# Adding up a guard's counts on VectorE after a small DMA, in place of an FP32 matmul on TensorE

## The chip, the cores and the metric

The kernel runs on one core of one Trainium2 chip. The metric is device time in microseconds (us) of one execution, and the figure given is the median over several runs. A profile of one execution stands beside it; its times count from the first to the last recorded instruction of the core (the span).

## What is computed

For 4 batches, 8 heads, 768 positions and a head width of 64 the reference does windowed attention with four sink positions and passes the result, with the heads side by side (512 columns), through a normalised two-layer block:

```python
scores = scale * np.matmul(q, k.transpose(0, 1, 3, 2))
keep = is_sink | in_window          # 4 sinks, a window of 128
a = np.exp(scores - max); a = a / (sum(a) + 1e-09)
x = np.matmul(a, v)                 # to [4, 768, 512]
xn = (x - mu) / np.sqrt(var + 1e-06) * g_ln
out = x + np.maximum(xn @ w_ch1, 0.0) @ w_ch2   # 512 -> 2048 -> 512
```

## The kernel before

**Tiles and stages.** The 3072 rows of the output are 24 tiles of 128 rows (`NT`), two of which make a chunk (`NC` = 12 chunks). Each tile is attended (scores L980, exponentials L998, values L953 to L969, reciprocals of the row sums L1021), normalised (L881 to L891) and transposed by a DMA (L577). Each chunk then goes through the two layers in `mlp(c)`: eight groups of first-layer matmuls `ph` (L1046), each followed by a ReLU on ScalarE (L1056), then for each tile i of the chunk sixteen second-layer matmuls `pc` in four groups `pc{t}{f}_{s}` (L1074), a VectorE instruction `o{t}{f}` that scales the sum and adds x (L1083), and a store of the tile to HBM, `st{t}{f}` (L1087). The last tile, 23, is cut into two halves of 256 columns: the first half's store is issued by ScalarE, the second half's by SyncE, and that one is the last store of the program (`order_last`, L1132).

**The guard.** The exponentials are taken without subtracting the row maximum, so a check runs at the end: `guard` (L1114 to L1116, VectorE) looks at all 24 x 8 reciprocals of each of the 128 partitions and leaves one count per partition in `n_bad`, 128 x 1. `gsum` (L1119) adds the 128 counts with an FP32 matmul against a column of ones, on TensorE, into one element of PSUM; `gflag` (L1121, VectorE) turns that element into the integer `flag`. At the end every engine reads `flag` into a register (`values_load`, L1159) and branches (L1161): over zero, the whole computation is done again by a slow general path; at zero, which is what happens here, the program ends. The last store on SyncE is put behind SyncE's read of the flag (L1160). `hold` (L1125) is a small FP32 matmul behind the last `o`.

**What sets the order.** Every step is an operation of `Plan` with a cost on each engine that may do it, a priority, and the buffers that it reads and writes. `Plan.run` plays the operations through with these costs and writes down the order of each engine; the instructions are then emitted in that order (L1152 to L1160), and each engine runs its own list in order. `gsum` has the priority `16.0 * NC + 0.7`, which puts it into the second-layer matmuls of tile 22, between the first and the second group of four (`pc220_0` and `pc220_1`). The four PSUM buffers `one` are shared by `ph`, `pc`, `gsum` and `hold` as they come free.

**Completion counters of DMAs.** Each DMA that SyncE or ScalarE issues takes the next of eight completion counters in turn, 0 to 7 and then 0 again; a consumer waits on the counter of its DMA. In the kernel before, the last few are: transpose of tile 23 counter 2, store of tile 20 counter 3, of tile 21 counter 4, of tile 22 counter 5, first half of tile 23 counter 6, second half 7.

**The end of the program.** After its branch SyncE goes through twelve waits, one instruction each, before it reports to the barrier that closes the program; in the profile they are the EVENT_SEMAPHORE rows of SyncE at L1196. Waits 1 to 4 name the counters of the GpSimd DMAs, two at a time. Waits 5 to 12 name the hardware DMA counters 0, 1, 2, ... 7 in this order, each beside a counter of an engine.

Of the kernel before, what the change touches and what calls it, by code (L numbers as in the profile page):

```python
# [7 lines left out]
FP32 = mybir.dt.float32  # L8
BF16 = mybir.dt.bfloat16
AF = mybir.ActivationFunctionType  # L10
ALU = mybir.AluOpType
# [185 lines left out]
def pe(us):  # L197
    return {"PE": (us, us + Plan.PE_DRAIN)}


def act(n):
    t = 0.065 + 0.000833 * n
    return (t, t + 0.105)


def dve(n, per=1.04):
    t = 0.067 + 0.001 * per * n
    return (t, t + 0.09)


def fix(occ, extra=0.09):
    return (occ, occ + extra)
# [10 lines left out]
HW_T = (0.10, 0.8, 0.8)  # L223
# [146 lines left out]
def kernel(  # L370
# [12 lines left out]
    nc = tc.nc  # L383
# [10 lines left out]
    NT = B * RB  # L394
    NC = B * RC
# [7 lines left out]
    P = Plan()  # L403
# [26 lines left out]
    def const(name, shape, dtype):  # L430
        return consts.tile(shape, dtype, name=name)
# [14 lines left out]
    w2 = [const(f"w2_{c}", [128, 4, DM], BF16) for c in range(4)]  # L446
    junk = nc.const_aps.tensor(1.0, [128, 512], BF16)
    rec, low = const("rec", [128, NT, H], FP32), const("low", [128, NT, H], FP32)
    n_bad, flag = const("n_bad", [128, 1], FP32), const("flag", [1, 1], mybir.dt.int32)
    g_s, g_r = const("g_s", [128, H, NS], FP32), const("g_r", [128, 3, H], FP32)  # L450
    ones_f = const("ones_f", [128, 1], FP32)
# [3 lines left out]
    Bc = {n: Buf(n) for n in names}  # L455
# [4 lines left out]
    def constant(name, eng, us, prio, emit, reads=(), **kw):  # L460
        return P.op(name, {eng: fix(us)}, prio, emit, reads=[Bc[r] for r in reads], **kw)

    V, G = nc.vector, nc.gpsimd
# [4 lines left out]
        out=ident_f, in_=ident_f, compare_op=ALU.not_equal, fill=1.0, base=0,  # L468
        pattern=[[-1, 128]], channel_multiplier=1), rw=[Bc["ident_f"]])
    constant("up1", "POOL", 0.3, -98, lambda e: G.affine_select(  # L470
        out=upper, in_=upper, compare_op=ALU.is_ge, fill=0.0, base=0,
# [36 lines left out]
    def negs(e):  # L508
# [7 lines left out]
        out=sel.rearrange("p (a b h) -> p a b h", a=2, b=2),  # L516
        in_=ident.rearrange("p (a b t h s) -> p t a b h s", a=2, b=2, h=2, s=NS)[:, 0],
        op=ALU.add, axis=mybir.AxisListType.X), ["ident"], writes=[Bc["sel"]])
# [8 lines left out]
         writes=[gr_b], dma=HW_T)  # L527
    P.op("gtt", pe(0.1), PAR["gtt"], lambda e: nc.tensor.transpose(gt_p.t[:, 0:NDM], g_rows, ident_f[0:NDM, 0:NDM]),
         reads=[gr_b, Bc["ident_f"]], writes=[gt_p])
    P.op("gtc", {"DVE": fix(0.07)}, PAR["gtt"] + 0.1, lambda e: V.tensor_copy(gt, gt_p.t[:, 0:NDM]), reads=[gt_p], writes=[Bc["gt"]])  # L530
    for h in range(H):
# [3 lines left out]
            reads=[Bc["vc"]], writes=[Bc["vcd"]], nb=3.5 + 0.55 * h)  # L535
    for b in range(B):
# [4 lines left out]
            reads=[Bc["vcd"], Bc["vc"], Bc["sel4" if b else "sel"]], writes=[Bvs[b]], nb=PAR["vs0"][1] if b == 0 else 40.0 * b)  # L541
# [7 lines left out]
    for c in range(4):  # L549
        sl = slice(512 * c, 512 * (c + 1))  # L550
        P.op(f"w1ld{c}", {"POOL": (0.75, 0.8)}, w1prio[c], lambda e, c=c, sl=sl: G.dma_start(
            w1[c], moe_w_ch1[:, sl].rearrange("(j p) n -> p j n", p=128)), writes=[Bw1[c]], dma=SW_W)
    for c in range(4):
        P.op(f"w2ld{c}", {"POOL": (0.75, 0.8)}, PAR["w2p"][c], lambda e, c=c: G.dma_start(
            w2[c], moe_w_ch2[512 * c:512 * (c + 1), :].rearrange("(t p) n -> p t n", p=128)),
            writes=[Bw2[c]], dma=SW_W)
# [471 lines left out]
    def mlp(c):  # L1028
        T = 16.0 * c + 8.0
        xnt = xnt_b[c]  # L1030
        h1 = []
        by_tile = c < PAR["by_tile"]
        for u in range(NH1 // 2):
            ph, hb = Buf(f"ph{c}_{u}", "one"), Buf(f"h{c}_{u}", "h1")

            def mm_t(e, u=u, ph=ph):
                for s in range(4):
                    for j in range(NDM):
                        nc.tensor.matmul(ph.t[:, 128 * s:128 * s + 128], lhsT=w1[u // 2][:, j, 128 * s:128 * s + 128],  # L1039
                                         rhs=xnt.t[:, j, 128 * (u % 2):128 * (u % 2) + 128], start=j == 0, stop=j == NDM - 1)  # L1040

            def mm(e, u=u, ph=ph):
                for s in range(2):
                    ht = 2 * u + s
                    for j in range(NDM):
                        nc.tensor.matmul(ph.t[:, 256 * s:256 * s + 256],  # L1046
                                         lhsT=w1[ht // 4][:, j, 128 * (ht % 4):128 * (ht % 4 + 1)],
                                         rhs=xnt.t[:, j, :], start=j == 0, stop=j == NDM - 1)
            pr = T + u + 0.5
            o = P.op(f"ph{c}_{u}", pe(0.944 if by_tile else 0.872), pr, mm_t if by_tile else mm, reads=[xnt_t[2 * c + u % 2] if by_tile else xnt, (Bw1 if c < PAR["x_by_dma"] else Bw1g)[u // 2]],  # L1050
                     writes=[ph], hold=[hb, xnt])
            last_use[u // 2] = [o]

            def rl(e, ph=ph, hb=hb):
                if e == "ACT":
                    nc.scalar.activation(hb.t, ph.t, AF.Relu)  # L1056
                else:
                    V.tensor_scalar_max(hb.t, ph.t, 0.0)
            P.op(f"rl{c}_{u}", {"ACT": act(512), "DVE": dve(512)}, pr - 3, rl, reads=[ph], writes=[hb])
            h1.append(hb)  # L1060
        T += 8
        for i in range(2):
            t = 2 * c + i
            b, r = t // RB, t % RB
            ot, st, rs, x = Buf(f"ot{t}", "ot"), xst_b[t], xst_b[t, "rs"], x_b[t]
            cuts = LAST_CUTS if t == NT - 1 else (0, DM)
            for f in range(len(cuts) - 1):
                pc, wd = Buf(f"pc{t}{f}", "one"), cuts[f + 1] - cuts[f]
                sl = slice(cuts[f], cuts[f + 1])
                for s in range(4):  # L1070
                    def mm(e, s=s, i=i, pc=pc, sl=sl, wd=wd):
                        for ii in range(4):
                            ht = 4 * s + ii
                            nc.tensor.matmul(pc.t[:, 0:wd],  # L1074
                                             lhsT=(h1[2 * s + i].t[:, 128 * ii:128 * ii + 128] if by_tile else
                                                   h1[ht // 2].t[:, 256 * (ht % 2) + 128 * i:256 * (ht % 2) + 128 * i + 128]),
                                             rhs=w2[s][:, ii, sl], start=ht == 0, stop=ht == NH1 - 1)
                    P.op(f"pc{t}{f}_{s}", pe(0.865 * wd / DM), T + 4 * i + s + 4 * f + 0.5, mm,
                         reads=[*([h1[2 * s + i]] if by_tile else h1[2 * s:2 * s + 2]), Bw2[s]], **({"writes": [pc]} if s == 0 else {"rw": [pc]}))
                oo = Buf(f"oo{t}{f}")  # L1080
                tail["ot"], tail["oo"] = ot, oo
                P.op(f"o{t}{f}", {"DVE": dve(wd, 1.14)}, T + 4 * i + 3.5, lambda e, sl=sl, pc=pc, wd=wd, ot=ot, st=st, x=x:
                     V.scalar_tensor_tensor(ot.t[:, sl], in0=pc.t[:, 0:wd], scalar=st.t[:, 16:17],  # L1083
                                            in1=x.t[:, sl], op0=ALU.mult, op1=ALU.add),
                     reads=[pc, st, rs, x], writes=[ot, oo])
                P.op(f"st{t}{f}", {"ACT" if len(cuts) - f in LAST_ACT else "SP": (0.54, 0.59)}, T + 4 * i + 3.6,
                     lambda e, sl=sl, ot=ot, b=b, r=r: (nc.sync if e == "SP" else nc.scalar).dma_start(  # L1087
                         out[b, 128 * r:128 * (r + 1), sl], ot.t[:, sl]),
                     reads=[ot, oo], dma=HW_S)

    last_use, tail = {}, {}
# [11 lines left out]
    for c in range(NC):  # L1103
        mlp(c)
        if c == PAR["x_by_dma"] - 1:
            for s in range(4):
                for j in range(NDM):
                    P.op(f"w1g{s}{j}", {"DVE": fix(0.26), "ACT": act(512)}, 16.0 * c + PAR["w1g"] + 2 * s + 0.1 * j,
                         lambda e, s=s, j=j: V.tensor_scalar_mul(w1[s][:, j, :], w1[s][:, j, :], gt[:, j:j + 1]) if e == "DVE" else
                         nc.scalar.mul(w1[s][:, j, :], w1[s][:, j, :], gt[:, j:j + 1]),  # L1110
                         reads=[Bw1[s], Bc["gt"]], writes=[Bw1g[s]], after=last_use[s])

    def guard(e):
        V.tensor_scalar(low, rec, LOW, HIGH, op0=ALU.max, op1=ALU.min)  # L1114
        V.tensor_tensor(low, low, rec, op=ALU.not_equal)
        V.tensor_reduce(out=n_bad, in_=low, op=ALU.add, axis=mybir.AxisListType.XY)  # L1116
    nb_b, pt_f, fl_b = Buf("n_bad"), Buf("ptf", "one"), Buf("flag")
    P.op("guard", {"DVE": fix(0.9)}, 1000.0, guard, reads=recs, writes=[nb_b])
    P.op("gsum", pe(0.06), 16.0 * NC + 0.7, lambda e: nc.tensor.matmul(  # L1119
        pt_f.t[0:1, 0:1], lhsT=n_bad, rhs=ones_f, start=True, stop=True), reads=[nb_b, Bc["ones_f"]], writes=[pt_f])  # L1120
    P.op("gflag", {"DVE": fix(0.1)}, 1000.0, lambda e: V.tensor_copy(flag, pt_f.t[0:1, 0:1]),  # L1121
         reads=[pt_f], writes=[fl_b])

    hl = Buf("hold", "one")
    P.op("hold", pe(0.06), 1000.0, lambda e: nc.tensor.matmul(  # L1125
        hl.t[0:1, 0:1], lhsT=tail["ot"].t[:, DM - 1:DM], rhs=ones_f, start=True, stop=True),
        reads=[tail["ot"], tail["oo"], Bc["ones_f"]], writes=[hl])
# [5 lines left out]
    t = PAR["t0"]  # L1133
    for o in order:
# [6 lines left out]
        if n > 0:  # L1141
            free = [(max([e_ for b_, e_ in banks[i].lives if b_ < t], default=0.0), i) for i in range(8)
                    if all(e_ < t or b_ > o.start + 0.3 for b_, e_ in banks[i].lives)]
            if free:
                i = min(free)[1]
                sizes = [512] * (n // 2) + [256] * (n % 2) if cold else [256] * n
                items.append((t + 0.001, -1, (sizes, pairs[i // 2][:, i % 2, :] if i < 4 else ones[i - 4])))
        t = o.start + occ * (2 if cold and not o.name.startswith("pm") else 1)
# [52 lines left out]
```

## Time and profile before

| what | value |
|---|---|
| median of 3 runs | 216.78 us (216.47 to 216.9) |
| the profiled execution's own time | 217.02 us |
| its span, first to last instruction | 215.5 us |
| TensorE busy / VectorE busy | 205.9 us / 115.3 us |
| granted TensorE clock | 1.000 |

Views of the profile used below: the page (busy times, the chain of work that ended last), the chain in order of time, the timeline (start, duration, engine, line, operation, with neighbouring instructions of a kind merged; a narrow stretch of time shows them nearly one by one), one line's instructions with their durations (min/median/max in ns) and their first and last start, and the DMA view. PE is TensorE's matmuls, PEld its weight loads, DVE VectorE, ACT ScalarE, POOL GpSimd, SP SyncE; a q behind a name is that engine's sequencer, where DMA issues, waits, register loads and branches are found. A matmul's duration includes its way through the array, so matmuls overlap in the records and their rate is read from their starts.

### The profile page before, as it was taken

The numbers are of one execution on the slowest core, as the hardware profiler recorded it, in microseconds if no ns is written. First come the engines' busy times: TensorE is split into PE (matmuls) and PEld (weight loads), VectorE is DVE, ScalarE is ACT, GpSimd is POOL, SyncE is SP. The second block draws the span as 40 slices with busy tenths as digits, with TensorE's granted clock in tenths as the row PEclk, the third lists the DMA queues.
The fourth block names the chain that finished last, engine by engine and source line by source line (L and its number), as shares of the span: only waits on it lengthen the run. The fifth ranks groups of instructions, "written<-read, shape, count | busy, mean of one in ns | idle before, by whom it ended". The sixth has DMA issues, their size and how long they took to land.

```text
span 215.5 us, 6660 instructions
## 1 busy us (share of the span) xinstructions
PE 205.9 (96%) x2743; PEld 144.1 (67%) x2765; DVE 115.3 (53%) x315; ACT 110.0 (51%) x178; POOL 111.8 (52%) x166
## 2 busy tenths in 40 slices
PE   7798899999999999999999999999999999999994
PEld 2467875765865875864865865864865865865853
DVE  5589875698445446446345446446355345444011
ACT  3796387496562562562562562562562562530610
POOL 7978632499972881871971981871971211201000
PEclk9999999999999999999999999999999999999999
DMA  5999999999999999799799899899799302202103
GB/s 156 187 190 205 193 206 192 167 180 132 154 187 169 123 125 145 87 175 151 123 115 170 112 147 145 111 122 168 111 141 149 80 3 76 73 0 76 49 2 105
DMA packets 104554, 28.04 MB, mean 130 GB/s; under 512 B 94788, under 2 KB 101576, under 8 KB 104520
## 3 DMA queue, kind: packets, MB, share of 16 engines
q0 software_dynamic: 69872, 13.18, 90.2%
q1 hardware_dynamic: 33448, 13.74, 35.7%
q10 hardware_dynamic: 1200, 0.66, 1.1%
q8 instruction: 22, 0.36, 0.7%
q14 instruction: 12, 0.10, 0.2%
HBM read 27.43 MB, written 6.29 MB: 156 GB/s over the span
## 4 chain that ended last, share of the span: by engine, by line
PE 88%; DVE 5%; DMA 3%; issue 2%; ACT 1%; ACTq 0%; DVEq 0%
PE one L1074 39%; PE one L1046 36%; PE pair L980 3%; DMA natf<-in_q_dram 3%; PE one L953 2%; PE one L960 2%; PE one L969 1%; DVE st L881 1%; DVE xnt L909 1%; PE one L988 1%; PE one L1039 1%; DVE x L873 1%; DVE xc L885 1%; PE pair L605 1%; PE pair L730 1%
## 5 line engine op out<-in xcount | busy, mean ns | idle before, releaser
L1074 PE MATMUL one<-w,h 128*128 128x512 bf16 (+1 forms) x378 | 84.5, 371 | 2.2 <-issue 1.6
L1056 ACT ACTIVATE h<-one 128x512 bf16<-128x512 f32 x93 | 55.6, 598 | 47.3 <-PE one L1046 42.6
L1046 PE MATMUL one<-xnt,w 128*128 128x256 bf16 x704 | 79.3, 273 | 0.0
L1046 PEld LDWEIGHTS <-w 128*128 128x128 bf16 x704 | 68.6, 98 | 10.4
L1074 PEld LDWEIGHTS <-h 128*128 128x128 bf16 x400 | 37.3, 98 | 39.6
L998 ACT ACTIVATE pe<-pair 128x768 bf16<-128x768 f32 x36 | 27.2, 809 | 41.0 <-PE pair L980 41.0
L645 POOL DMA_DIRECT2D vn<-in_v_dram x59 | 38.7, 695 | 10.9 <-DMA w<-in_moe_w_ch_dram 6.8
L890 POOL TENSOR_SCALAR st<-st 128x1 f32<-128x1 f32 x24 | 8.9, 369 | 62.4 <-DVE st L883 61.9
L1021 DVE RECIPROCAL rec<-one 128x4 f32<-128x4 f32 x36 | 6.4, 178 | 62.5 <-PE one L969 51.1
L1083 DVE SCALAR_TENSOR_TENSOR ot<-one,st,x 128x512 f32<-128x512 f32 (+1 forms) x25 | 18.2, 727 | 13.9 <-PE one L1074 9.0
L891 POOL TENSOR_TENSOR st<-st,mhalf 128x1 f32<-128x1 f32 x24 | 17.0, 707 | 2.0
L881 DVE BATCH_NORM_STATS2 st<-x 128x6 f32<-128x512 bf16 x24 | 16.7, 695 | 0.8
L1023 DVE TENSOR_TENSOR x<-one,rec 128x256 bf16<-128x256 f32 x36 | 15.3, 425 | 1.2
L703 POOL DMA_DIRECT2D nat<-in_k_dram x16 | 14.9, 932 | 1.9 <-DMA natp<-in_q_dram 1.6
L703 POOL DMA_DIRECT2D nat<-in_q_dram x16 | 14.3, 905 | 0.0
L1003 DVE TENSOR_TENSOR pe<-pe,band 128x768 bf16<-128x768 bf16 x24 | 12.2, 552 | 0.0
L885 DVE TENSOR_SCALAR xc<-x,st 128x512 bf16<-128x512 bf16 x24 | 9.3, 387 | 0.9
L980 PE MATMUL pair<-qT,kT 64*64 64x128 bf16 (+1 forms) x528 | 9.2, 204 | 0.0
L953 PEld LDWEIGHTS <-pe 128*128 128x128 bf16 (+1 forms) x144 | 6.2, 97 | 2.9 <-issue 0.8
L778 ACT ACTIVATE pe<-pair 128x1024 bf16<-128x1024 f32 (+1 forms) x8 | 7.1, 916 | 1.8 <-PE pair L730 1.4
L1039 PE MATMUL one<-xnt,w 128*128 128x128 bf16 x128 | 8.0, 220 | 0.0
L980 PEld LDWEIGHTS <-kT 64*64 64x64 bf16 x528 | 7.2, 108 | 0.4 <-ACT w L1110 0.4
(112 smaller groups left out, 165.7 us busy)
## 6 DMA issues: line engine op xcount, KB each, us to landing
out_dram<-ot SPq DMA_DIRECT2D x23, 256.0 KB
w<-in_moe_w_ch_dram POOLq DMA_DIRECT2D x8, 512.0 KB, 14.5
nat<-in_k_dram POOLq DMA_DIRECT2D x16, 128.0 KB, 5.1
nat<-in_q_dram POOLq DMA_DIRECT2D x16, 128.0 KB, 5.6
vn<-in_v_dram POOLq DMA_DIRECT2D x44, 32.0 KB, 6.0
vn<-in_v_dram POOLq DMA_DIRECT2D x15, 64.0 KB, 6.3
natp<-in_k_dram POOLq DMA_DIRECT2D x3, 256.0 KB, 14.3
vn<-in_v_dram POOLq DMA_DIRECT2D x6, 128.0 KB, 9.2
```

Of the source, the lines that this page charges most:

```text
L645: P.op(f"vld{t}_{i}", {"POOL": (0.8, 0.85)}, prio + 0.001 * i, lambda e, p0=p0, n=n, hs=hs, src=src: G.dma_start(m.t[p0:p0 + n, hs, 0:64], ...
L703: lambda e, nat=nat, ap=ap: G.dma_start(nat.t, ap), writes=[nat], dma=SW, after=gate(c))
L881: P.op(f"bn{t}", {"DVE": fix(0.60)}, d + 0.12, lambda e: V.bn_stats(st.t[:, 8:14], x.t), reads=[x], writes=[st, mv])
L891: G.tensor_tensor(st.t[:, 16:17], st.t[:, 17:18], mhalf, op=ALU.pow)),
L980: nc.tensor.matmul(pps[u].t[64 * g:64 * g + 64, h2, col + c0:col + c0 + n], lhsT=kt.t[rs, hp, k0:k0 + 64], rhs=qT.t[rs, hp, q0:q0 + n], st ...
L998: nc.scalar.activation(pes[j].t.rearrange("p a b -> p (a b)")[:, 0:768].rearrange("p (a b) -> p a b", a=2), pps[j].t[:, :, 0:384], AF.Exp, ...
L1003: V.tensor_mul(at_s, at_s, band[j] if r > 1 else edge[r][j].unsqueeze(1).to_broadcast([128, 4, 192]))
L1023: P.op(f"x{t - 1}{u}", {"DVE": dve(256)}, d + 0.051 + 0.002 * u, lambda e, u=u, rc=rc, pv=pv: V.tensor_tensor(x.t[:, 256 * u:256 * u + 256 ...
L1046: nc.tensor.matmul(ph.t[:, 256 * s:256 * s + 256], lhsT=w1[ht // 4][:, j, 128 * (ht % 4):128 * (ht % 4 + 1)], rhs=xnt.t[:, j, :], start=j ...
L1056: nc.scalar.activation(hb.t, ph.t, AF.Relu)
L1074: nc.tensor.matmul(pc.t[:, 0:wd], lhsT=(h1[2 * s + i].t[:, 128 * ii:128 * ii + 128] if by_tile else h1[ht // 2].t[:, 256 * (ht % 2) + 128 ...
L1083: V.scalar_tensor_tensor(ot.t[:, sl], in0=pc.t[:, 0:wd], scalar=st.t[:, 16:17], in1=x.t[:, sl], op0=ALU.mult, op1=ALU.add),
```

## The change

The matmul `gsum` goes. A DMA `gmove`, issued by SyncE, carries the 128 counts from 128 partitions into 128 neighbouring elements of one partition, and `gflag` becomes two VectorE instructions: a reduction of these 128 elements and the conversion to an integer. The new `gflag` is ordered behind `o220`, the VectorE step of tile 22 (`tail["sum", NT - 2]`).

```diff
+    n_bad_t, n_sum = const("n_bad_t", [1, 128], FP32), const("n_sum", [1, 1], FP32)
...
-                P.op(f"o{t}{f}", {"DVE": dve(wd, 1.14)}, T + 4 * i + 3.5, lambda e, sl=sl, pc=pc, wd=wd, ot=ot, st=st, x=x:
+                tail["sum", t] = P.op(f"o{t}{f}", {"DVE": dve(wd, 1.14)}, T + 4 * i + 3.5, lambda e, sl=sl, pc=pc, wd=wd, ot=ot, st=st, x=x:
...
-    P.op("gsum", pe(0.06), 16.0 * NC + 0.7, lambda e: nc.tensor.matmul(
-        pt_f.t[0:1, 0:1], lhsT=n_bad, rhs=ones_f, start=True, stop=True), reads=[nb_b, Bc["ones_f"]], writes=[pt_f])
-    P.op("gflag", {"DVE": fix(0.1)}, 1000.0, lambda e: V.tensor_copy(flag, pt_f.t[0:1, 0:1]),
-         reads=[pt_f], writes=[fl_b])
+    nt_b = Buf("n_bad_t")
+    P.op("gmove", {"SP": (0.54, 0.59)}, 1000.0, lambda e: nc.sync.dma_start(n_bad_t[0:1, :], n_bad[:, 0:1]),
+         reads=[nb_b], writes=[nt_b], dma=HW_T)
+
+    def total(e):
+        V.tensor_reduce(out=n_sum, in_=n_bad_t, op=ALU.add, axis=mybir.AxisListType.X)
+        V.tensor_copy(flag, n_sum)
+    P.op("gflag", {"DVE": fix(0.2)}, 1000.0, total, reads=[nt_b], writes=[fl_b], after=[tail["sum", NT - 2]])
```

In the built program the rest of every engine's list keeps its order. TensorE loses the one instruction at L1119, and the two halves of tile 23 move to another PSUM buffer each. On SyncE `gmove` stands between the transpose of tile 23 and the store of tile 20; on VectorE the two new instructions stand between `o220` and `o230`, where one stood before between `o210` and `o220`. As `gmove` takes counter 3, each later store takes the next counter: tile 20 counter 4, 21 counter 5, 22 counter 6, the first half of tile 23 counter 7, the second half counter 0.

More of the change, by code (lines that the diff above doesn't have):

```diff
@@ L1116, in guard @@
         V.tensor_reduce(out=n_bad, in_=low, op=ALU.add, axis=mybir.AxisListType.XY)
-    nb_b, pt_f, fl_b = Buf("n_bad"), Buf("ptf", "one"), Buf("flag")
+    nb_b, fl_b = Buf("n_bad"), Buf("flag")
     P.op("guard", {"DVE": fix(0.9)}, 1000.0, guard, reads=recs, writes=[nb_b])
-    P.op("gsum", pe(0.06), 16.0 * NC + 0.7, lambda e: nc.tensor.matmul(
-        pt_f.t[0:1, 0:1], lhsT=n_bad, rhs=ones_f, start=True, stop=True), reads=[nb_b, Bc["ones_f"]], writes=[pt_f])
-    P.op("gflag", {"DVE": fix(0.1)}, 1000.0, lambda e: V.tensor_copy(flag, pt_f.t[0:1, 0:1]),
-         reads=[pt_f], writes=[fl_b])
+    nt_b = Buf("n_bad_t")
[5 more added lines that the diff above has]
+    P.op("gflag", {"DVE": fix(0.2)}, 1000.0, total, reads=[nt_b], writes=[fl_b], after=[tail["sum", NT - 2]])
     hl = Buf("hold", "one")
```

## The prediction

> **What bounds the kernel now.** I read the page first, its busy times and its chain of work that ended last:
>
> ```profile
> span 215.5 us, 6660 instructions
> PE 205.9 (96%) x2743; PEld 144.1 (67%) x2765; DVE 115.3 (53%) x315; ACT 110.0 (51%) x178; POOL 111.8 (52%) x166
> ...
> PE 88%; DVE 5%; DMA 3%; issue 2%; ACT 1%; ACTq 0%; DVEq 0%
> ```
>
> TensorE is busy for 96% of the span and carries 88% of the chain. Whatever is taken out of TensorE's list moves all that follows it, so the next view is the chain in order of time, its last pieces (start, us, what):
>
> ```profile
> 205.09 0.22 PE one L1074
> 205.31 0.05 issue
> 205.36 0.60 PE one L1074 x2
> 205.96 0.12 PE one L1119 x2
> 206.07 6.20 PE one L1074 x44
> ...
> 212.37 0.50 DVE ot L1083
> ```
>
> The removed matmul, L1119, lies on the chain. Behind it come 6.20 us of matmuls without a gap, then VectorE's last instruction, then the last store. The end after that store does not appear in the chain as pieces of its own, so I looked up what SyncE does there, at L1196 (count, durations in ns, first and last start). The rows are those of four stretches of time: all until 214.5, until 214.06, from 214.06 to 214.5, and behind 214.5.
>
> ```profile
> L1196 SPq EVENT_SEMAPHORE  x11: 28/28/28, 213.8 to 214.4; - x11
> ...
> L1196 SPq EVENT_SEMAPHORE  x4: 28/28/28, 213.8 to 214.0; - x4
> ...
> L1196 SPq EVENT_SEMAPHORE  x7: 28/28/28, 214.1 to 214.4; - x7
> ...
> L1196 SPq EVENT_SEMAPHORE  x1: 28/28/28, 214.6 to 214.6; - x1
> L1196 SPq DRAIN  x1: 13/13/13, 214.7 to 214.7; - x1
> ```
>
> These are the twelve closing waits. Eleven start between 213.8 and 214.4, ten steps in 0.6 us: 0.06 us for one, although there is nothing left to wait for in them. The twelfth comes at 214.6, some 0.1 us later than this rhythm would bring it. By the program it names counter 7, that of the last store, so it is the one that really waits. The drain follows a step later and the barrier closes the program at 215.5. So the end is: last matmul, VectorE, last store, its landing, and then **no** further wait, because the store's counter stands last in the row.
>
> **What the removed matmul costs.** The chain puts down 0.12 us for it. The starts of its neighbours tell more. The timeline in narrow stretches:
>
> ```profile
> 205.36 0.60 PE L1074 MATMUL one<-w,h 128*128 128x512 bf16 x2
> ...
> 205.57 0.38 PE L1074 MATMUL one<-w,h 128*128 128x512 bf16 x1
> 205.88 0.09 PEld L1119 LDWEIGHTS one<-ones_f,n_bad 128*1 128x1 f32 x2 [0.42 <-ACT h L1056]
> 205.88 0.19 PE L1119 MATMUL one<-ones_f,n_bad 128*1 128x1 f32 x2
> ...
> 206.01 0.60 PE L1074 MATMUL one<-w,h 128*128 128x512 bf16 x2
> ...
> 206.01 0.82 PE L1074 MATMUL one<-w,h 128*128 128x512 bf16 x3
> ```
>
> Two merged matmuls last 0.60 and three 0.82, so one more costs 0.22; the starts 205.36 and 205.57 say 0.21. The matmul behind 205.57 was therefore due at 205.79 and starts at 206.01: **0.22 us lost**, nearly twice the 0.12 of the chain. The row puts the idle time ahead of L1119 down to a ReLU of L1056; I take that label for a coincidence, since by the program L1119 needs a PSUM buffer that an older ReLU, two before the last, has read.
>
> What is late next once it goes? The last ReLU and VectorE's steps:
>
> ```profile
> 205.19 0.60 ACT L1056 ACTIVATE h<-one 128x512 bf16<-128x512 f32 x1 [0.28 <-PE one L1046]
> ...
> 206.11 0.15 DVE L1121 CAST flag<-one 1x1 int32<-1x1 f32 x1 [7.16 <-PE one L1119]
> 208.86 0.75 DVE L1083 SCALAR_TENSOR_TENSOR ot<-one,st,x 128x512 f32<-128x512 f32 x1 [2.61 <-PE one L1074]
> 210.72 0.48 DVE L1083 SCALAR_TENSOR_TENSOR ot<-one,st,x 128x256 f32<-128x256 f32 x1 [1.11 <-PE one L1074]
> 212.37 0.48 DVE L1083 SCALAR_TENSOR_TENSOR ot<-one,st,x 128x256 f32<-128x256 f32 x1 [1.16 <-PE one L1074]
> ```
>
> The last ReLU ends at 205.79. Its first reader is the fifteenth of tile 22's sixteen matmuls; at 0.215 each from 204.93 on it is due at 207.9, two microseconds later. So nothing takes the place of the gap, and I take the whole 0.22 us, with 0.12 as the lower bound. The three VectorE steps each wait for PE and come 0.22 earlier: 208.64, 210.50, 212.15.
>
> **What is added, and what hides it.** First the DMA. On SyncE it stands behind the transpose of tile 23 and ahead of the store of tile 20; it needs the counts of L1116:
>
> ```profile
> 193.75 1.20 SPq L577 DMA_TRANSPOSE xnt<-xc  x1
> ...
> 194.32 0.35 DVE L1116 TENSOR_REDUCE n_bad<-low 128x1 f32<-128x192 f32 x1
> 194.74 0.75 DVE L1083 SCALAR_TENSOR_TENSOR ot<-one,st,x 128x512 f32<-128x512 f32 x1
> ...
> 195.52 0.34 SPq L1087 DMA_DIRECT2D out_dram<-ot  x1
> ```
>
> The counts are there at 194.67, the transpose has been issued at 194.95, and the store waits for VectorE until 195.49. Issuing a store of 128 rows takes 0.34 us and fits into that hole of 0.54. The longest issue among the stores bounds it from above; then the store of tile 20 would start 1.0 us late, with nobody waiting for it before the end. The transpose is ahead of the new DMA and keeps its place.
>
> ```profile
> L1087 SPq DMA_DIRECT2D out_dram<-ot x24: 332/337/1519, 41.1 to 212.9; - x24
> ...
> w<-in_moe_w_ch_dram POOLq DMA_DIRECT2D x8, 512.0 KB, 14.5
> ...
> vn<-in_v_dram POOLq DMA_DIRECT2D x44, 32.0 KB, 6.0
> ```
>
> When does it land? No such DMA, 128 runs of four bytes between partitions, is in this trace. The nearest by size is the 32 KB load, 6.0 us from issue to landing in a busy stretch; the slowest of all is a weight load, 14.5 us. VectorE reaches the reduction at 209.39 (208.64 + 0.75), so from 195.0 there are 14.4 us of cover. Even the slowest would be a bare 0.1 us late, inside the next gap. I cost it at nothing.
>
> The rule in the Trainium skill that speaks against this change is in "DMA: Bandwidth & Descriptors", section "Anatomy of one DMA — SWDGE (gpsimd) path": any DMA, however small, pays some 2 us, most of it for completion. By it the sum, if the DMA stood on the chain, would be 1.8 us worse; behind 14 us of cover it changes nothing, and no row of this trace times so small a transfer.
>
> Then VectorE's two instructions. The reduction lies between the conversion's 0.15 us and the 0.35 us of L1116, which reads 192 elements per partition where this one reads 128; I take 0.3. With the conversion and two steps to start them it makes about 0.5 us, from 209.4 to 209.9, and `o230` is not due before 210.50. Should it run over, `o230` may be late by 1.1 us more before it touches `o231` at 212.15. Nothing again.
>
> The flag is thereby late, at 209.9 and no longer at 206.3. Its readers:
>
> ```profile
> L1159 POOLq TENSOR_LOAD <-flag x1: 498/498/498, 206.3 to 206.3; - x1
> L1159 SPq TENSOR_LOAD <-flag x1: 516/516/516, 210.0 to 210.0; - x1
> ...
> L1159 ACTq TENSOR_LOAD <-flag x1: 473/473/473, 211.7 to 211.7; - x1
> L1159 DVEq TENSOR_LOAD <-flag x1: 546/546/546, 212.4 to 212.4; - x1
> L1159 PEldq TENSOR_LOAD <-flag x1: 490/490/490, 212.9 to 212.9; - x1
> ```
>
> SyncE read it at 210.0, behind the store of tile 22, and has some 2 us before its last store, started at 212.9 in the row of the stores and due at 212.7 now. It does not feel the difference. ScalarE, VectorE and TensorE read later still. Only GpSimd moves, by 3.6 us; that is a rival below.
>
> **What is moved: the counter of the last store.** The added DMA takes a counter, so the last store's is no longer 7 but 0, and 0 is named in the fifth closing wait, not the twelfth. SyncE now comes to the fifth wait at 213.86 (the first of the seven in the row from 214.1, less 0.22), stands there until the store has landed, and only then walks through the seven waits that are left, at 0.06 each, satisfied or not. The store itself lands 0.22 us earlier. The sum from the landing on:
>
> - landing earlier: -0.22
> - seven waits behind it, 7 x 0.06: +0.42 (by rounding of the rows between 0.35 and 0.49)
> - together **+0.20 us**: the drain at 214.9 where it was 214.7, the end at 215.7.
>
> Between ends this is +0.13 to +0.37. On the profiled execution's own 217.02 us it gives 217.22; this execution is 0.24 over the median of the runs shown, 216.78, and the difference carried over makes 216.98. I forecast **217.0 us**: the gain on TensorE is real and is handed back in the closing waits.
>
> **The rivals.** *The full gain arrives.* If waits that are already satisfied cost nothing behind one that has blocked, or the counter order does not hold the end, the time is 216.78 - 0.22 = 216.56. For it: the chain shows the 0.22 plainly. Against it: eleven waits with nothing to wait for took 0.06 each in the rows above.
>
> *The gap on TensorE stays.* If the 0.22 us were a wait for something that the next matmul meets as well, only the closing waits would be left: 216.78 + 0.42 = 217.20. For it is the label of the row, which names a ReLU; against it, that the matmuls behind ran on at once while the last ReLU had ended at 205.79, before L1119.
>
> *GpSimd closes the program late.* This is the one that ends slower:
>
> ```profile
> L1196 POOLq EVENT_SEMAPHORE  x4: 17/17/17, 214.8 to 215.4; - x4
> L1196 POOLq DRAIN  x3: 44/103/1380, 208.3 to 215.3; - x3
> ...
> L1161 POOLq INC_SWDGE_SEM  x1: 512/512/512, 207.8 to 207.8; - x1
> ```
>
> From its read of the flag at 206.3 GpSimd needs until 208.3 + 1.38 = 209.7, which is 3.4 us, then it waits for the others until 214.8. Started at 209.9 it is done at 213.3, with 1.7 us to spare before the 215.0 that my sum needs. It decides once the stretch grows by more than 1.7 us, and from there on each microsecond is one on the end: with the drain and the semaphore step (1.38 and 0.51) twice as long beside the stores it would be 217.2, with the whole stretch twice as long 218.7. Against it: the same steps run on the same idle engine, and nothing else was behind them before.
>
> **How the numbers follow.** 0.2% is 0.43 us, about what a measurement of this kernel can tell from no change (three runs spread from 216.47 to 216.9). Forecast, +0.20: 0.68. Full gain, -0.22: 0.14. Gap stays, +0.42: 0.08. GpSimd late, mostly by over half a microsecond: 0.10. The first two lie within the bound but for the spread of a measurement; the third lies on its edge, the fourth beyond. Slower by over 0.2%: 0.10, half of 0.08, and 0.06 out of the forecast's tail, 0.20. Faster: 0.05, out of the full gain's tail. Within: 0.75. The range takes in the full gain at its lower end and the nearer part of the late GpSimd at its upper: 216.45 to 217.45.
>
> **What would show it.** In the profile after: L1074 without a gap between its fourth and fifth matmul of tile 22, and VectorE's last three steps 0.2 us earlier; the last store issued at 212.7; on SyncE five closing waits up to about 214.4, with a gap before the fifth, and seven behind it at 0.06; GpSimd's read of the flag at 209.9 and its drain done by 213.5. The forecast is wrong if the twelfth wait follows the landing at once, or if `o230` or the last store starts later than its matmuls allow.

## The result, and the profile after

| | before | after |
|---|---|---|
| median of 22 runs each | 216.66 us (216.33 to 217.09) | 216.91 us (216.58 to 217.84) |
| ratio, 95% interval | | 1.0013 [1.0007, 1.0019] |
| the profiled execution | 217.02 us, span 215.5 | 216.81 us, span 215.3 |

The changed kernel is slower by 0.25 us (0.15 to 0.41 by the interval), where +0.20 was forecast. The one profiled execution of it is a little shorter than that of before. This is no contradiction: the two had come 0.6 us apart before the first added instruction (the counts start to be summed at 194.32 before and at 193.72 after), in work that the change leaves alone, and the runs of one kernel spread by more than that. So the two traces are compared from that point on.

The chain after, in order of time (start, us, what), from the first matmul of tile 22:

```profile
204.50 6.96 PE one L1075 x48
211.46 0.03 issue
211.49 0.02 DVEq L1084
211.51 0.04 issue
211.55 0.50 DVE ot L1084
```

Lines past the new tile stand one lower, so L1075 is L1074 of before. All 48 matmuls are now one piece. Before, VectorE's last step started 7.28 us after the first piece of tile 22 (205.09 to 212.37); now it is 7.05 (204.50 to 211.55). The gain of 0.23 us on TensorE is there.

What was added, in the timeline after:

```profile
193.72 0.35 DVE L1117 TENSOR_REDUCE n_bad<-low 128x1 f32<-128x192 f32 x1
194.15 0.75 DVE L1084 SCALAR_TENSOR_TENSOR ot<-one,st,x 128x512 f32<-128x512 f32 x1
194.45 0.53 SPq L1121 DMA_DIRECT2D n_bad_t<-n_bad  x1
195.07 0.54 SPq L1088 DMA_DIRECT2D out_dram<-ot  x1
...
208.04 0.75 DVE L1084 SCALAR_TENSOR_TENSOR ot<-one,st,x 128x512 f32<-128x512 f32 x1 [9.69 <-PE one L1075]
208.71 0.26 DVE L1125 TENSOR_REDUCE n_sum<-n_bad_t 1x1 f32<-1x128 f32 x1
...
209.01 0.14 DVE L1126 CAST flag<-n_sum 1x1 int32<-1x1 f32 x1
209.90 0.48 DVE L1084 SCALAR_TENSOR_TENSOR ot<-one,st,x 128x256 f32<-128x256 f32 x1 [0.75 <-PE one L1075]
```

The DMA's issue takes 0.53 us and holds the store of tile 20 until 195.07, 0.17 after VectorE has finished that tile; nobody waits for it. The reduction follows its VectorE step without a pause, and the flag is ready at 209.15, with 0.75 us of idle VectorE behind it. GpSimd, which reads the flag at 209.2, has finished its long drain at 212.6:

```profile
L1200 POOLq DRAIN  x3: 44/103/1380, 211.2 to 215.0; - x3
```

And the end, SyncE's closing waits after, in two stretches:

```profile
L1200 SPq EVENT_SEMAPHORE  x4: 28/28/28, 213.0 to 213.2; - x4
...
L1200 SPq EVENT_SEMAPHORE  x8: 27/28/28, 214.0 to 214.4; - x8
L1200 SPq DRAIN  x1: 13/13/13, 214.4 to 214.4; - x1
```

Before it was eleven in a row and one that stood. Now four pass, the fifth stands from 213.3 to 214.0, and seven more follow it in 0.4 us with nothing to wait for. The last store's landing is no longer the end of the row.

### The profile page after: what moved, and what is told of

Read it like the earlier page. It is cut to its first block, busy times and chain, and to the rows that moved or that the text cites. A ratio compares the mean times of both kernels' runs of the same rounds, so it can differ in the third digit from the quotient of the medians.

```text
span 215.3 us, 6681 instructions
## 1 busy us (share of the span) xinstructions
PE 207.5 (96%) x2763; PEld 144.0 (67%) x2763; DVE 114.9 (53%) x316; ACT 110.0 (51%) x178; POOL 111.0 (52%) x166
## 4 chain that ended last, share of the span: by engine, by line
PE 89%; DVE 5%; DMA 3%; ACT 1%; issue 1%; ACTq 0%; DVEq 0%
PE one L1075 40%; PE one L1047 36%; PE pair L981 3%; DMA natf<-in_q_dram 3%; PE one L954 2%; PE one L961 2%; PE one L970 1%; DVE st L882 1%; DVE xnt L910 1%; PE one L989 1%; PE one L1040 1%; DVE x L874 1%; PE pair L606 1%; PE pair L731 1%; DVE pe L782 1%
## 5 line engine op out<-in xcount | busy, mean ns | idle before, releaser
L1075 PE MATMUL one<-w,h 128*128 128x512 bf16 (+1 forms) x400 | 87.2, 371 | 0.0
L1075 PEld LDWEIGHTS <-h 128*128 128x128 bf16 x400 | 37.4, 98 | 39.8
L891 POOL TENSOR_SCALAR st<-st 128x1 f32<-128x1 f32 x24 | 8.4, 351 | 60.1 <-DVE st L884 59.4
L892 POOL TENSOR_TENSOR st<-st,mhalf 128x1 f32<-128x1 f32 x24 | 16.5, 688 | 2.0
L886 DVE TENSOR_SCALAR xc<-x,st 128x512 bf16<-128x512 bf16 x24 | 8.8, 365 | 0.9
```

What stands on the lines that cost most here:

```text
L892: G.tensor_tensor(st.t[:, 16:17], st.t[:, 17:18], mhalf, op=ALU.pow)),
L1075: nc.tensor.matmul(pc.t[:, 0:wd], lhsT=(h1[2 * s + i].t[:, 128 * ii:128 * ii + 128] if by_tile else h1[ht // 2].t[:, 256 * (ht % 2) + 128 ...
```

## The experiments

Two theories were set against each other. **Place of the counter:** the 0.22 us of TensorE are gained, and lost again because the added DMA shifts the last store's counter from the twelfth closing wait to the fifth. **Added work:** the DMA, the reduction or the wait for them cost the time. All ratios are against runs of the kernel before on the same chip; "counter" is that of the last store.

| kernel | guard's matmul | counter, place | median us | before, same chip | ratio [95% interval] |
|---|---|---|---|---|---|
| changed | none | 0, 5th | 216.91 | 216.66 | 1.0013 [1.0007, 1.0019] |
| e1 DMA by GpSimd | none | 7, 12th | 216.54 | 216.70 | 0.9993 [0.9984, 1.0002] |
| e2 no DMA | none | 7, 12th | 216.57 | 216.70 | 0.9996 [0.9987, 1.0004] |
| e3 before + 1 DMA | FP32 | 0, 5th | 217.09 | 216.70 | 1.0019 [1.0009, 1.0029] |
| e4 changed + 7 DMAs | none | 7, 12th | 216.43 | 216.70 | 0.9986 [0.9978, 0.9995] |
| e5 changed + 3 DMAs | none | 3, 8th | 216.74 | 216.71 | 1.0003 [0.9993, 1.0014] |
| e6 before, BF16 | BF16, 1 column | 7, 12th | 216.71 | 216.71 | 1.0003 [0.9994, 1.0011] |
| e7 before + 8 DMAs | FP32 | 7, 12th | 216.80 | 216.71 | 1.0005 [0.9994, 1.0015] |
| e8 before, BF16, wide | BF16, 128 columns | 7, 12th | 216.69 | 216.86 | 0.9994 [0.9980, 1.0007] |

**e1: GpSimd issues the small DMA.**

```diff
-    P.op("gmove", {"SP": (0.54, 0.59)}, 1000.0, lambda e: nc.sync.dma_start(n_bad_t[0:1, :], n_bad[:, 0:1]),
-         reads=[nb_b], writes=[nt_b], dma=HW_T)
+    P.op("gmove", {"POOL": (0.9, 0.93)}, 1000.0, lambda e: G.dma_start(n_bad_t[0:1, :], n_bad[:, 0:1]),
+         reads=[nb_b], writes=[nt_b], dma=SW_Q)
```

> The changed kernel with one edit: GpSimd issues the small DMA and SyncE does not, so the last store is back on completion counter 7, named in the twelfth closing wait. DMA, reduction and conversion are all still there. Theory (place of the counter): only the 0.22 us of TensorE are left, so 0.2 us faster than before (216.44 against 216.66) and some 0.4 faster than the changed kernel; in the profile SyncE's twelfth closing wait is the one that stands. Rival (the added DMA or VectorE work costs the time, by whatever way): as slow as the changed kernel, 0.2 to 0.3 over before.

216.54 against 216.70: 0.16 under before, where the changed kernel was 0.25 over (0.9993 against 1.0013). Its interval reaches just past no change, but lies clear of the changed kernel's. The chain from the first matmul of tile 22 on is that of the changed kernel to 0.01 us (206.23 to 213.28, 7.05), and the twelfth wait stands again. The profiled execution was the longest of the 13, 217.96 us; only its end is read here.

```profile
206.23 6.96 PE one L1075 x48
...
213.28 0.49 DVE ot L1084
```

```profile
L1200 SPq EVENT_SEMAPHORE  x11: 28/28/28, 214.7 to 215.3; - x11
...
L1200 SPq EVENT_SEMAPHORE  x1: 28/28/28, 215.5 to 215.5; - x1
L1200 SPq DRAIN  x1: 13/13/13, 215.6 to 215.6; - x1
```

The same DMA, reduction and conversion as in the changed kernel, and no loss: against added work.

**e2: no DMA at all.**

```diff
-    P.op("gmove", ...
...
-        V.tensor_reduce(out=n_sum, in_=n_bad_t, op=ALU.add, axis=mybir.AxisListType.X)
+        V.tensor_copy(n_sum, n_bad[0:1, 0:1])
...
```

> The changed kernel without the small DMA: the flag is made from the count of partition 0 alone, by two one-element VectorE copies; the counts of the other 127 partitions are left out. Counter 7 holds the last store again. Both theories expect the gain of TensorE alone, 0.2 us faster than before (216.44). Were the gain not real (the gap on TensorE costs nothing), it would be 216.66 within 0.1. Against the run with GpSimd's DMA it says what the DMA and the reduction cost beside the counter: nothing by the theory.

0.13 us under before, 0.03 from e1. (`gflag` now reads the counts themselves and waits for no DMA.) The DMA and the reduction cost nothing that these runs can see. On its own the 0.13 is not clear of zero either.

**e3: before, with one DMA more.**

```diff
+    n_bad_t = const("n_bad_t", [1, 128], FP32)
...
+    P.op("gmove", {"SP": (0.54, 0.59)}, 1000.0, lambda e: nc.sync.dma_start(n_bad_t[0:1, :], n_bad[:, 0:1]),
+         reads=[nb_b], writes=[Buf("n_bad_t")], dma=HW_T)
```

> The kernel before, FP32 matmul and all, with the same small DMA added on SyncE, whose result nobody reads. The last store moves from counter 7 to counter 0. Theory: seven waits behind the landing at 0.06 us, 0.4 us slower than before (217.1); in the profile five closing waits, a gap before the fifth, then seven in a row. Rival (the DMA is only slow because VectorE waits for it): no difference to before, since nobody waits for it.

0.39 us slower than before, from one 512-byte transfer that nobody waits for. Its closing waits show the same picture as the changed kernel's:

```profile
L1199 SPq EVENT_SEMAPHORE  x4: 28/28/28, 213.3 to 213.5; - x4
...
L1199 SPq EVENT_SEMAPHORE  x8: 28/28/28, 214.4 to 214.8; - x8
```

**e4: the changed kernel with seven DMAs more.**

```diff
+    n_more = const("n_more", [1, 7, 128], FP32)
...
+    for i in range(7):
+        P.op(f"more{i}", {"SP": (0.54, 0.59)}, 1001.0 + i, lambda e, i=i: nc.sync.dma_start(n_more[0:1, i, :], n_bad[:, 0:1]),
+             reads=[nb_b], writes=[Buf(f"more{i}")], dma=HW_T)
```

> The changed kernel with seven more small DMAs of the same kind on SyncE, whose results nobody reads, six of them behind the store of tile 20 and one behind that of tile 21. The eight DMAs together bring the last store back to counter 7. Theory: more work and yet faster, 0.2 us under before (216.44), 0.4 under the changed kernel. Rival (each added DMA costs): slower than the changed kernel, by up to seven times what one costs, 0.3 us and more over before.

0.27 us faster than before, the one version whose interval lies wholly under both kernels. Eight DMAs bring the counter round to 7, and the row of waits is the old one:

```profile
L1204 SPq EVENT_SEMAPHORE  x11: 28/28/28, 213.0 to 213.6; - x11
...
L1204 SPq EVENT_SEMAPHORE  x1: 28/28/28, 213.8 to 213.8; - x1
L1204 SPq DRAIN  x1: 13/13/13, 213.8 to 213.8; - x1
```

More work and a shorter time: of the two theories only the place of the counter allows it.

**e5: three more in place of seven** (`range(3)`).

> The changed kernel with three more small DMAs on SyncE that nobody reads: the last store is on counter 3, named in the eighth closing wait, so four waits stand behind the landing instead of seven or none. Theory (0.06 us for each wait behind the landing): -0.22 + 4 x 0.06 = +0.02, so as fast as before within 0.1, between the changed kernel (+0.25) and the one with seven more (-0.27); from the landing to the end of the span 1.21 us, where counter 7 shows 0.97 and counter 0 1.39. Rival (something about counter 0 itself, or about any counter but 7, costs 0.4): a full step, either -0.2 or +0.2.

+0.03 us, between the two ends and where four waits of 0.06 put it; from the landing to the end of the span the trace has the 1.21 us that were expected. Seven pass, the eighth stands, four follow:

```profile
L1204 SPq EVENT_SEMAPHORE  x7: 28/28/28, 213.0 to 213.4; - x7
...
L1204 SPq EVENT_SEMAPHORE  x5: 28/28/28, 214.1 to 214.3; - x5
```

The trace shows the place; the times alone (interval 0.9993 to 1.0014) would not rule out a step of -0.15.

**e7: before, with eight DMAs more** (the loop of e4 with `range(8)`, put into the kernel before).

> The kernel before with eight small DMAs on SyncE that nobody reads, in the same places as the eight of the changed kernel with seven more; eight bring the last store back to counter 7. Theory: nothing changes, 0.0 to before within 0.1, since the DMAs lie beside other work; against that other run it leaves the matmul alone as the difference, 0.2 us. Rival (each DMA costs on its own): 0.3 us and more over before, as one of them did.

+0.09, within 0.1 as expected, and clear of the 0.39 that one DMA cost in e3 only by its middle (the intervals overlap). With e4 it is the same pair as before and e1: no matmul, 0.36 us less (-0.27 against +0.09), more than the 0.22 of the theory, which lies within what the two intervals allow.

**e6: is it FP32?** The prediction left open why the matmul costs 0.22 us and not the 0.12 of the chain.

```diff
-    n_bad, flag = const("n_bad", [128, 1], FP32), const("flag", [1, 1], mybir.dt.int32)
+    n_bad, flag = const("n_bad", [128, 1], BF16), const("flag", [1, 1], mybir.dt.int32)
...
-        pt_f.t[0:1, 0:1], lhsT=n_bad, rhs=ones_f, start=True, stop=True), reads=[nb_b, Bc["ones_f"]], writes=[pt_f])
+        pt_f.t[0:1, 0:1], lhsT=n_bad, rhs=junk[:, 0:1], start=True, stop=True), reads=[nb_b, Bc["ones_f"]], writes=[pt_f])
```

> The kernel before with the counts in BF16 (they are whole numbers up to 192) and the matmul against a BF16 one: one weight load and one pass on TensorE, no DMA, counter 7 kept. It tells what of the 0.22 us belongs to FP32. If the cost is that an FP32 matmul does not let its weight load run ahead, the gap shrinks to under 0.1 us and the kernel is 0.1 to 0.2 us faster than before. If any one-column matmul in the stream costs as much, the gap stays at 0.2 and the time at that of before.

No change in time, and in the timeline the gap stands though `gsum` has one weight load and one pass only:

```profile
204.88 0.59 PE L1074 MATMUL one<-w,h 128*128 128x512 bf16 x2
205.40 0.08 PEld L1120 LDWEIGHTS <-n_bad 128*1 128x1 bf16 x1 [0.42 <-issue]
205.40 0.16 PE L1120 MATMUL one<-const-bfloat16-1.0,n_bad 128*1 128x1 bf16 x1
205.50 0.11 PEld L1074 LDWEIGHTS <-h 128*128 128x128 bf16 x2
205.50 0.39 PE L1074 MATMUL one<-w,h 128*128 128x512 bf16 x1
```

The two matmuls of the first row start at 204.88 and, a step of 0.215 on, at 205.09; the next was due at 205.31 and starts at 205.50. The load itself is as short as others (0.08), but it starts at 205.40, 0.09 us after the matmul before has streamed. And the load behind it, of 128 columns, starts only at 205.50, together with its own matmul and another 0.10 after the small one. The 0.19 us are these two late loads. FP32 is not the cause; in the kernel before its second pass adds 0.03 (205.88 to 205.91).

**e8: the same sum with wide weights** (the diff is against e6).

```diff
-        pt_f.t[0:1, 0:1], lhsT=n_bad, rhs=junk[:, 0:1],
+        pt_f.t[:, 0:1], lhsT=junk[:, 0:128], rhs=n_bad,
...
```

> The kernel before with BF16 counts as in the last run but with the operands changed over: a 128x128 field of ones is loaded as weights and the counts stream through as one column, so every partition gets the sum and the flag is read from partition 0. No DMA, counter 7 kept. The BF16 run with one column of weights kept the gap of 0.2 us, so FP32 is not its cause. If it is the narrow weight load (one column, which started only when the matmul before had streamed, where loads of 128 columns start a whole matmul ahead), the gap goes down to the 0.05 us or so of one more short matmul, and the kernel is 0.1 to 0.2 us faster than before. If any short matmul between the long ones costs a drain, the gap stays at 0.2 and the time at that of before.

```profile
205.15 0.10 PEld L1120 LDWEIGHTS <-const-bfloat16-1.0 128*128 128x128 bf16 x1
205.37 0.17 PE L1120 MATMUL one<-n_bad,const-bfloat16-1.0 128*128 128x1 bf16 x1
205.37 0.12 PEld L1074 LDWEIGHTS <-h 128*128 128x128 bf16 x2
205.39 0.38 PE L1074 MATMUL one<-w,h 128*128 128x512 bf16 x1
```

The load starts at 205.15, together with the matmul ahead of it, the load behind it at 205.37, together with the short matmul, and the short matmul delays the next by 0.02 to 0.03 us (205.37 to 205.39). So nearly all of the 0.22 us was the two late weight loads. The time is 0.17 under before, with an interval that reaches past no change: the trace shows the effect, the time only points the same way.

**e9: 64 columns, and e10: FP32 with 128 columns.** One profile each: `lhsT=junk[:, 0:64]` in e8, and `lhsT=ident_f, rhs=n_bad` in FP32 in the kernel before. The single times, 216.65 and 216.77 us beside 216.62 for before, tell nothing.

> The kernel before with BF16 counts streaming through 64 columns of ones (128 columns left a gap of 0.03 us, one column a gap of 0.19). One look at the trace. If only full loads of 128 columns start ahead, the gap is 0.15 us or more and the weight load starts when the matmul before has streamed; if one column is the special case, it is 0.03 and the load starts a matmul ahead. The time alone (0.2 us in a single run) tells nothing.

> The kernel before with FP32 kept but the operands changed over: the FP32 identity, 128 columns, is the weights, and the counts stream through, so that the flag is the count of partition 0 alone; the others are left out. One look at the trace. If FP32 has a price of its own beside the narrow load, there is a gap again, 0.1 us and more, with the weight loads behind the matmul before; if width alone decides, the loads start ahead and the gap is 0.06, two short passes.

The timeline of e9, then that of e10:

```profile
205.29 0.10 PEld L1120 LDWEIGHTS <-const-bfloat16-1.0 128*64 128x64 bf16 x1 [0.42 <-issue]
205.29 0.19 PE L1120 MATMUL one<-n_bad,const-bfloat16-1.0 128*64 128x1 bf16 x1
205.41 0.11 PEld L1074 LDWEIGHTS <-h 128*128 128x128 bf16 x2
205.42 0.39 PE L1074 MATMUL one<-w,h 128*128 128x512 bf16 x1
```

```profile
205.19 0.41 PEld L1119 LDWEIGHTS one<-n_bad,ident_f 128*128 128x128 f32 x2
205.40 0.28 PE L1119 MATMUL one<-n_bad,ident_f 128*128 128x1 f32 x2
205.43 0.21 PEld L1074 LDWEIGHTS <-h 128*128 128x128 bf16 x2
205.54 0.38 PE L1074 MATMUL one<-w,h 128*128 128x512 bf16 x1
```

With 64 columns the load waits again, until 205.29, 0.31 after the matmul before it started (204.98 in the trace), and the next long matmul comes 0.22 late; its load of 128 columns waits too, until 205.41. In FP32 with 128 columns it starts ahead, at 205.19, and the two passes delay the next matmul by 0.14 (205.40 to 205.54). That is more than the 0.06 expected from width alone: FP32 has a price of its own, 0.11 at this width, though its loads start ahead.

These runs do not tell a narrow load from a load of another shape than the one before it. The rows of the same traces do. The load of 128 columns behind the narrow one is as late as the narrow one (205.50 in e6, 205.41 in e9). And where 64-column loads follow one another, as at L598 in the kernel before, they do start ahead; by 12.05 five have started and three of their matmuls:

```profile
11.96 0.19 PEld L598 LDWEIGHTS <-natp 128*64 128x64 bf16 x5 [0.21 <-issue]
11.96 0.30 PE L598 MATMUL one<-ident,natp 128*64 128x128 bf16 x3
```

In the whole trace after, the shape (rows by columns) changes from one load to the next 79 times, and in 78 of them the new load starts no more than 0.005 us ahead of its own matmul; behind a load of its own shape a load of 128 x 128 does so in 9 of 1472 cases. So the change of shape goes with the late load, once on the way to the one column and once on the way back.

## Why the prediction was right

**The matmul's price, -0.22.** Right: 7.28 us became 7.05 between the same two points. That it had to be read from the starts of its neighbours and not from the 0.12 of the chain was right too; why, only e6 to e10 showed: 0.09 us until the one-column load starts, 0.03 for the second FP32 pass, 0.10 until the next load of 128 columns starts. The prediction had no account of this; it took the gap as it stood in the rows. The kernel's own `Plan` does: it puts 0.095 us (`SWITCH`) between operations of another `mode`, which follows the shape of the weights, but `gsum` is entered with the mode of the 128-column matmuls around it. The label of that row, a ReLU, was the coincidence it was taken for: e6 has the same idle 0.42 with "issue" as its end.

**The DMA and VectorE's two steps, nothing.** Right as far as these times tell: e1 and e2 are within 0.03 us of each other, and e4, with eight such DMAs on SyncE, is no slower. The reduction was put at 0.3 us and took 0.26. The issue on SyncE was put at 0.34 and took 0.53, within the bounds. The rule of the Trainium skill ("DMA: Bandwidth & Descriptors", section "Anatomy of one DMA — SWDGE (gpsimd) path") that even a small DMA pays some 2 us agrees with this case. The section speaks of DMAs that GpSimd issues: in e1, where GpSimd issues it, the transfer is complete 2.02 us after its issue began (196.11 to 198.13); issued by SyncE in the changed kernel, 1.96 us after (194.45 to 196.41). Of the 14 us of cover it used two. The prediction's price for it on the chain, 1.8 us, leaves the counter out; with 2 us more its own sum would have come to +2.2.

**The counter's place, +0.42.** Right in mechanism, and in size within what the runs can tell. Without the matmul the place makes 0.41 us (+0.25 in the changed kernel, -0.16 in e1), with it 0.39 (e3). In the traces the seven waits take 0.4 (214.0 to 214.4 after, 214.4 to 214.8 in e3). The sum, +0.20, came out at +0.25.

**The rivals.** The full gain does not arrive: waits that are already satisfied cost their 0.06 behind one that has stood. The gap did not stay on TensorE. GpSimd finished at 212.6, 1.9 us before it was needed at 214.5; this rival deserved less than its 0.10.

One term was not in the sum: the time from the last store's issue to its landing is no constant. From issue to the wait that stood it was 1.7 us before and in e1, e4 and e7, 1.8 in e2 and e8, 1.9 after and in e9 and e10, 2.0 in e3, e5 and e6. It moves a single profiled execution as much as the whole change does. The trace notes the landing in sixteen updates of the counter. In all twelve profiles fifteen of them are in 1.66 to 1.71 us after the issue; the last follows 0.02 to 0.04 us later in the quick ones and 0.10 to 0.25 later in the others, with counter 7 (0.25 in e6) as well as with 0 (0.17 after, 0.24 in e3) and 3 (0.25 in e5). So a slow landing needs no other counter than 7, and the medians' 0.41 and 0.39 ask for no more than the 0.42 of the waits; why one update comes late stays open.

## What to carry to other kernels

Follow a change to the very end of the program: when the work there is a row of waits that one engine walks through one by one, what counts is how many stand behind the one that really waits, and a DMA added or removed anywhere earlier, if it takes one of these counters, can change that place. Here one DMA on SyncE did (e3), and the same DMA on GpSimd did not and kept the gain (e1). A gain on the busiest engine is safe only when the steps behind the last result are counted as well. And before a small matmul is moved off TensorE, try it with its operands changed over, so that its weights have the shape of its neighbours': in BF16, 128 columns of weights and the short operand streaming left 0.03 us of the gap in the trace, in FP32 0.14; that the time follows was not clear of zero (e8).

## What the runs showed of the hardware that was not expected

A weight load of 128 columns behind another of 128 starts while the matmul before it is still running (205.15 against a matmul that hands over at 205.37, e8). Between loads of 128 columns, loads of 1 or 64 columns started about 0.1 us after that matmul had streamed (205.40 where 205.31 was due, e6), the next load of 128 columns came about 0.1 us late as well (205.50, e6), and the stream lost 0.2 us, whether FP32 or BF16. The Trainium skill says in "TensorE: Matmul & The Clock Gate", section "Architectural detail: the array is 16× 32×32, not 1× 128×128", that the queue can pull weight loads ahead of matmuls in flight; these traces agree where a load has the shape of the one before it (205.15 in e8, L598 before) and show none pulled ahead where the shape changes (78 of 79 times after).

A satisfied wait on SyncE is shown with 0.028 us but takes 0.06 of the engine's time, by the step between starts, in every one of these profiles, also directly behind a wait that has stood.
